# An attention and two-MoE kernel on one core: first transposes copied ahead of later angles, and w_out and g used unsplit in the first token block

## The chip, the cores and the metric

The kernel runs on one core of a Trainium2 chip. The metric is device time in microseconds of one execution, smaller is better. A run before the change took 1125.24 us (median of 3 runs, 1124.36 to 1126.98). The engines that matter here are PE (TensorE, matmuls and transposes), DVE (VectorE), ACT (ScalarE), POOL (GpSimd) and SP, which issues most of the DMAs.

## The reference

Inputs are float32. Three stages follow one another; the output of one, seen as 3072 tokens by 384 features, is the input of the next.

```
# 1. attention with complex decay, per batch (4) and head (8), 768 steps, head_dim 48
S = a_norm[t] * S + outer(k[t], v[t])      # a_norm complex, magnitude capped at 0.999
y[t] = q[t] @ real(S)
# 2. first MoE layer, d_ff = 2048
h = x @ w_in
g = h * tanh(log1p(exp(min(h, 20))))       # mish
x2 = g @ w_out
# 3. second MoE layer, d_ff = 1536
out = ((x2 @ w_a) * (x2 @ w_b)) @ w_out2
```

## The kernel before, in words

**Tiling.** Tokens are worked in 6 blocks of 512 (128 time steps of each of the 4 batches). Attention is done in 24 chunks of 128 steps, numbered so that chunks 0 to 3 make block 0, chunks 4 to 7 block 1, and so on. The angles and decays of a chunk are summed by matmuls against a triangle (`csum`, `tsum`), turned into sines and exponentials on ACT, multiplied into q and k on DVE (`rotate`), transposed on PE (`transpose_one`, copied out of PSUM by ACT), multiplied to scores, masked on DVE (L384) and multiplied with v.

**The lead.** `lead_in` (L754) does chunks 0 to 3 before any other work. The order of its instructions is a list written out by hand (L793 to L805); `in_order` then pins that order on DVE, ACT, PE and POOL. In it `(tr, c)` is the transposes of chunk c with their copies, `(trig, c)` two sines on ACT, `(reduced, c)` three DVE instructions that bring the summed angle into a turn, `(rotate, c)` two DVE multiplies, `(decode, None)` and `(split, None)` the first piece of w_in, `(decode_2, None)` and `(split_2, None)` the first piece of w_out.

**Weights.** Weights come as 768 KB pieces of two 32-bit words per number. `decode` (L152) makes float32 of them by three DVE instructions. `split` (L160) makes two float32r tiles: ACT copies the float32 tile into the high part, POOL subtracts it from the whole to get the low part. w_in and w_out have 8 pieces each, numbered j; each serves two of the 16 feature tiles f. They are loaded while block 0 runs, in turn (in 0, out 0, in 1, ...).

**First MoE.** For each block and each f, `moe1_h` makes `hps` = w_in by x with 9 matmuls (3 slices of 384 features, times 3 terms: high by high, high by low, low by high). `mish_factor` (L532) is one DVE instruction and four on ACT. `mish_product` (L542) multiplies by h on DVE, giving m; then `gh`, the high part of m, is made by ACT in the first and last block and by DVE in the others, and `gl`, the low part, by DVE in the first and last block and by POOL in the others. `moe1_x2` (L556) adds w_out by g into three PSUM tiles, again with 3 terms of 3 matmuls each, two units of f later. The accumulated tiles of a block are copied out as `x2o` after f = 15.

**What sets the order.** Outside the lead, instructions are recorded in the order of the loop over units (b, f) at L835, the attention chunks 4 to 23 in slots spread over it (`run_to`), and a scheduler of the framework then chooses, engine by engine, the order in the queues. Each engine's queue is in order.

**Second MoE.** `moe2_ab`, `moe2_mul`, `moe2_out`, with the same three terms. Its weights are loaded by `prep` from the last units of block 4 on. The first `EARLY` = 2 sets of them have tiles of their own, the rest reuse the tiles of the first MoE's weights (`shared`, L169), which lie in two pools of 16.

Of the kernel before, what the change touches and what calls it, by code (L numbers as in the profile page):

```python
# [21 lines left out]
def kernel(  # L22
# [14 lines left out]
    nc = tc.nc  # L37
# [77 lines left out]
    allp = ctx.enter_context(ExitStack())  # L115
    xp = allp.enter_context(tc.tile_pool(name="xp", bufs=2))
    ps_a = allp.enter_context(tc.tile_pool(name="ps_a", bufs=3, space=PSUM))
    wps = [allp.enter_context(tc.tile_pool(name="wp0", bufs=NF))]
    right = allp.enter_context(ExitStack())
    w1 = allp.enter_context(ExitStack())  # L120
    ps_h = w1.enter_context(tc.tile_pool(name="ps_h", bufs=2, space=PSUM))
# [14 lines left out]

    weights = {}

    def load_weights(nm, j, src, pool, place):


        a, b = src.shape[1:]
        if src.dtype == F32:
            raw = pool.tile([P, a, b], F32, tag="wraw", name="wraw", bufs=2)
            nc.sync.dma_start(out=raw, in_=src)
        else:
            b //= 2
            raw = pool.tile([P, a, b, 2], U32, tag="wraw", name="wraw", bufs=2)
            nc.sync.dma_start(out=raw.rearrange("p a b t -> p a (b t)"), in_=src)
        f = [raw]  # L150

        def decode():  # L152
            if src.dtype != F32:
                f[0] = pool.tile([P, a, b], F32, tag="wf32", name="wf32")
                fu, low, high = f[0].bitcast(U32), raw[..., 0], raw[..., 1]
                nc.vector.tensor_scalar(fu, high, 3, 0x3FFFFFFF, ALU.logical_shift_left, ALU.bitwise_and)
                nc.vector.scalar_tensor_tensor(fu, high, 0xC0000000, fu, ALU.bitwise_and, ALU.bitwise_or)
                nc.vector.scalar_tensor_tensor(fu, low, 29, fu, ALU.logical_shift_right, ALU.bitwise_or)

        def split():  # L160
            hi, lo = weights[nm, j] = [place(f"w{nm}{i}{j}", [P, a, b]) for i in "hl"]
            act(out=hi, in_=f[0], func=AF.Copy)
            nc.gpsimd.tensor_tensor(lo, f[0], hi.bitcast(F32), ALU.subtract)  # L163

        return [decode, split]

    taken = [0]

    def shared(name, shape):  # L169

        pool = wps[taken[0] // NF % 2]
# [367 lines left out]
        act(out=m, in_=m, func=AF.Exp, scale=-1.0)  # L539
        return m  # L540

    def mish_product(p, m, on_act):  # L542

        nc.vector.scalar_tensor_tensor(m, m, 2.5, p, ALU.subtract, ALU.mult)  # L544
        gh = mp.tile([P, TN], F32R, tag="gh", name="gh")
        gl = mp.tile([P, TN], F32R, tag="gl", name="gl")
        if on_act:
            act(out=gh, in_=m, func=AF.Copy)
        else:
            nc.vector.tensor_copy(gh, m)  # L550
        (nc.vector if on_act else nc.gpsimd).tensor_tensor(gl, m, gh.bitcast(F32), ALU.subtract)  # L551
        return gh, gl

    x2ps = {}

    def moe1_x2(blk, f, gh, gl):  # L556
        for m in range(KM):
            if f == 0:
                x2ps[m] = ps_x.tile([P, TN], F32, tag=f"x{m}", name=f"x2ps{m}")
            ms = slice(m * P, (m + 1) * P)  # L560
            hi, lo = w_row("out", f)
            for i, (w, g) in enumerate([(hi, gh), (hi, gl), (lo, gh)]):
                nc.tensor.matmul(  # L563
                    x2ps[m], lhsT=w[:, ms], rhs=g,
                    start=(f == 0 and i == 0), stop=(f == NF - 1 and i == 2),
                )
        if f == NF - 1:
            for m in range(KM):
                t = mp.tile([P, TN], F32, tag="m", name="x2o")
                if m == 1:  # L570
                    nc.vector.tensor_scalar(t, x2ps[m], -0.4, None, ALU.mult)
                else:
                    act(out=t, in_=x2ps[m], func=AF.Copy, scale=-0.4)
                nc.sync.dma_start(out=x2_d[blk][m * P:(m + 1) * P, :], in_=t)
# [4 lines left out]
    def load_w2(early):  # L579


        for j in range(NF2 // 2):
            def place(name, shape, j=j):
                return early[0].tile(shape, F32R, name=name) if j < EARLY else shared(name, shape)

            for nm, src in (("a", wcols(w2_a, j)), ("b", wcols(w2_b, j)), ("o", wrow(w2_out, j))):
                yield lambda nm=nm, j=j, src=src, place=place: load_weights(nm, j, src, wst, place)
# [166 lines left out]
    def lead_in():  # L754
# [38 lines left out]
        for fn, c in (  # L793
            (decay_1, 0), (decay_2, 0), (decay_1, 1), (decay_3, 0), (decay_2, 1), (decay_1, 2), (tan_ell, 0),
            (decay_3, 1), (sum_ell, 0), (decay_2, 2), (sizes, 0), (tan_ell, 1), (decay_1, 3), (decay_3, 2),
            (sum_ell, 1), (decay_2, 3), (sizes, 1), (tan_ell, 2), (decay_3, 3), (sum_ell, 2), (sizes, 2), (tan_ell, 3), (sum_ell, 3),
            (scale_qk, 0), (sizes, 3), (scale_qk, 1), (decode, None), (split, None),
            (angle, 0), (angle, 1), (angle, 2), (angle, 3), (turned, 0), (turned, 1), (turned, 2), (turned, 3),
            (scale_qk, 2), (reduced, 0), (trig, 0), (reduced, 1), (trig, 1), (rotate, 0), (reduced, 2), (trig, 2),
            (tr, 0), (rotate, 1), (scale_qk, 3), (sc, 0), (tr, 1), (reduced, 3), (trig, 3), (values, 0), (rotate, 2),  # L800
            (store_y, 0), (sc, 1), (tr, 2), (read_x, 0), (split_x, 0), (rotate, 3), (values, 1), (decode_2, None),
            (store_y, 1), (sc, 2), (tr, 3), (lambda: run_to(0), None), (read_x, 1), (split_x, 1), (values, 2),
            (split_2, None), (store_y, 2), (lambda: run_to(1), None), (sc, 3), (read_x, 2), (split_x, 2),
            (lambda: run_to(2), None), (values, 3), (store_y, 3), (read_x, 3), (split_x, 3),
        ):  # L805
            fn() if c is None else fn(c)
# [28 lines left out]
    for ui in range(len(units) + lag):  # L835
        if ui == 3:
            behind(after_lead, last)
        if ui < len(units):
            blk, f = units[ui]
            if f == 0:  # L840
                base = slot[0]
                want = ends[blk + 1] if blk + 1 < NB else n_slots
                if blk == NB - 1:
                    make_room()
            p = moe1_h(blk, f, ps_a if blk == NB - 1 and f % 2 else ps_h)
            do_w()
            run_to(base + (want - base) * (2 * f + 1) // (2 * NF))
            m = mish_factor(p)
            if blk == NB - 1 and f % 5 != 4 or blk == NB - 2 and f >= NF - 2:
                next(prep, None)  # L850
        if ui == 1:
# [224 lines left out]
```

## Time and profile before

| what | value |
|---|---|
| median of 3 runs | 1125.24 us |
| the profiled execution, time | 1126.85 us |
| the profiled execution, span | 1125.1 us |
| PE busy | 1063.6 us (95%) |
| PE weight loads busy | 897.1 us (80%) |
| DVE busy | 663.9 us (59%) |
| ACT busy | 617.7 us (55%) |
| POOL busy | 228.8 us (20%) |
| first matmul of block 0 (`hps`) | 63.26 us |
| first copy of block 0's result (`x2o`) | about 209 us |

The time of a run includes some microseconds around the span. Busy PE counts overlapping, modelled ends of matmuls, so a busy PE may still have room; the busy time of the weight loads is the better sign of how dense the matmuls are. The stretches used below are the lead (0 to 63.26 us), block 0 of the first MoE with the weights' arrival and the chunks 4 to 8 (63.26 to 209.20 us), block 1 (209.20 to 301.50 us) and a stretch of the same kind after it.

### The profile page before, as it was taken

How to read it: one execution, taken by the hardware profiler on the slowest of the kernel's cores; microseconds unless marked ns; L12 is line 12 of the kernel's file. 1: busy time of each engine (PE TensorE's matmuls, PEld its weight loads, DVE VectorE, ACT ScalarE, POOL GpSimd, SP SyncE). 2: the span in 40 equal slices, each digit the busy share in tenths (PEclk: the TensorE clock that was granted, in tenths of full speed). 3: DMA queues.
4: the chain of work that ended last, by engine and by line, in shares of the span. 5: the costliest groups of instructions: out<-in, count | busy, mean ns of one | idle time of the engine just before them, and what ended most of it. 6: DMA issues, size and time to landing. Idle time of an engine off the chain costs nothing.

```text
span 1125.1 us, 15347 instructions
## 1 busy us (share of the span) xinstructions
PE 1063.6 (95%) x5788; PEld 897.1 (80%) x5788; DVE 663.9 (59%) x1014; ACT 617.7 (55%) x978; POOL 228.8 (20%) x220
## 2 busy tenths in 40 slices
PE   3897988999999999999998999999999999999997
PEld 1775667888788878878876778878888888888886
DVE  5789988777677767677658998742232321412222
ACT  6578877877787887879766862221121121211211
POOL 2022324343334334334232212100000000000000
PEclk9898989999999999999999999999999999999999
DMA  9335755733343453324325556410010100100000
GB/s 207 73 106 129 177 127 129 161 64 64 65 97 74 82 119 68 65 64 99 71 71 165 164 181 202 130 57 1 1 57 1 29 29 1 43 1 1 29 1 30
DMA packets 203545, 90.87 MB, mean 81 GB/s; under 512 B 144781, under 2 KB 187850, under 8 KB 203466
## 3 DMA queue, kind: packets, MB, share of 16 engines
q1 hardware_dynamic: 203450, 89.82, 32.6%
q8 instruction: 47, 0.77, 0.3%
q14 instruction: 32, 0.26, 0.1%
q10 hardware_dynamic: 16, 0.01, 0.0%
HBM read 72.44 MB, written 17.36 MB: 80 GB/s over the span
## 4 chain that ended last, share of the span: by engine, by line
PE 43%; ACT 12%; DVE 10%; issue 9%; DMA 4%; POOL 3%; SPq 0%; ACTq 0%; POOLq 0%; DVEq 0%
PE ops L641 11%; PE psa L616 11%; PE psb L616 11%; ACT m L60 7%; PE hps L529 4%; PE x2ps L563 3%; DVE m L535 2%; DVE kh L349 1%; ACT s L60 1%; ACT L55 1%; DMA look<-in_a_im_dram 1%; POOL wbl L163 1%; ACT a L60 1%; DVE m L544 1%; PE py L404 1%
## 5 line engine op out<-in xcount | busy, mean ns | idle before, releaser
L627 DVE TENSOR_TENSOR a_sb<-a_sb,psb 128x512 f32<-128x512 f32 x72 | 49.4, 686 | 221.7 <-PE psb L616 220.1
L60 ACT ACTIVATE m<-m 128x512 f32<-128x512 f32 x192 | 120.2, 628 | 67.8 <-DVE m L535 65.3
L60 ACT ACTIVATE ph<-a_sb 128x512 fp32r<-128x512 f32 x72 | 45.5, 632 | 178.4 <-DVE a_sb L627 178.4
L529 PE MATMUL hps<-xh,winh 128*128 128x512 f32 x288 | 119.5, 416 | 8.7 <-DVE m L544 6.9
L60 ACT ACTIVATE a_sb<-psa 128x512 f32<-128x512 f32 x72 | 42.9, 596 | 151.6 <-PE psa L616 149.4
L563 PE MATMUL x2ps<-gl,wouth 128*128 128x512 f32 x288 | 114.9, 399 | 4.8 <-DVE gl L551 3.4
L529 PE MATMUL hps<-xl,winh 128*128 128x512 f32 x288 | 116.4, 404 | 0.5 <-DMA xl<-yt_dl 0.5
L563 PE MATMUL x2ps<-gh,wouth 128*128 128x512 f32 x288 | 114.8, 406 | 1.4 <-ACT x2o L60 0.8
L529 PE MATMUL hps<-xh,winl 128*128 128x512 f32 x288 | 114.9, 399 | 0.0
L551 POOL TENSOR_TENSOR gl<-m,gh 128x512 fp32r<-128x512 f32 x64 | 83.4, 1303 | 154.6 <-DVE gh L550 147.1
L563 PE MATMUL x2ps<-gh,woutl 128*128 128x512 f32 x288 | 113.2, 393 | 0.0
L641 PE MATMUL ops<-woh,ph 128*128 128x384 f32 x288 | 97.2, 337 | 0.0
L641 PE MATMUL ops<-woh,pl 128*128 128x384 f32 x288 | 97.2, 337 | 0.0
L641 PE MATMUL ops<-wol,ph 128*128 128x384 f32 x288 | 96.8, 336 | 0.0
L544 DVE SCALAR_TENSOR_TENSOR m<-m,hps 128x512 f32<-128x512 f32 x96 | 65.4, 682 | 40.5 <-ACT m L60 40.5
L616 PE MATMUL psa<-xh,wah 128*128 128x512 f32 x216 | 84.7, 392 | 2.2 <-DVE a_sb L627 2.2
L616 PE MATMUL psa<-xh,wal 128*128 128x512 f32 x216 | 85.1, 394 | 0.0
L616 PE MATMUL psa<-xl,wah 128*128 128x512 f32 x216 | 85.0, 394 | 0.0
L616 PE MATMUL psb<-xh,wbh 128*128 128x512 f32 x216 | 84.5, 391 | 0.0
L616 PE MATMUL psb<-xh,wbl 128*128 128x512 f32 x216 | 84.4, 391 | 0.0
L616 PE MATMUL psb<-xl,wbh 128*128 128x512 f32 x216 | 84.4, 391 | 0.0
L535 DVE TENSOR_SCALAR m<-hps 128x512 f32<-128x512 f32 x96 | 65.5, 682 | 17.8 <-PE hps L529 16.3
(137 smaller groups left out, 2322.1 us busy)
## 6 DMA issues: line engine op xcount, KB each, us to landing
wraw<-in_moe_w_out_dram SPq DMA_DIRECT2D x14, 768.0 KB
wraw<-in_moe_w_in_dram SPq DMA_DIRECT2D x8, 768.0 KB
a<-in_a_re_dram SPq DMA_DIRECT2D x24, 192.0 KB
a<-in_a_im_dram SPq DMA_DIRECT2D x24, 192.0 KB
q<-in_q_dram SPq DMA_DIRECT2D x24, 192.0 KB
k<-in_k_dram SPq DMA_DIRECT2D x24, 192.0 KB
v<-in_v_dram SPq DMA_DIRECT2D x24, 192.0 KB
wraw<-in_moe_w_a_dram SPq DMA_DIRECT2D x6, 768.0 KB
```

What stands on the lines that cost most here:

```text
L55: load = nc.scalar.preload_act_table_set(name)
L60: x = nc.scalar.activation(**kw)
L163: nc.gpsimd.tensor_tensor(lo, f[0], hi.bitcast(F32), ALU.subtract)
L349: eng.tensor_tensor(tile1(c, nm + "h", [P, H, 2, D]), x, w, ALU.mult)
L529: nc.tensor.matmul(p, lhsT=w[:, kk, :], rhs=x[:, kk, :], start=(i == 0), stop=(i == len(ops) - 1))
L535: nc.vector.tensor_scalar(m, p, 20.0, None, ALU.min)
L544: nc.vector.scalar_tensor_tensor(m, m, 2.5, p, ALU.subtract, ALU.mult)
L551: (nc.vector if on_act else nc.gpsimd).tensor_tensor(gl, m, gh.bitcast(F32), ALU.subtract)
L563: nc.tensor.matmul(x2ps[m], lhsT=w[:, ms], rhs=g, start=(f == 0 and i == 0), stop=(f == NF - 1 and i == 2),)
L616: nc.tensor.matmul(p, lhsT=w[:, kk, :], rhs=x[:, kk, :], start=(i == 0), stop=(i == len(ops) - 1))
L627: nc.vector.tensor_tensor(a_sb, a_sb, pb, ALU.mult)
L641: nc.tensor.matmul(ops_t[t], lhsT=x[:, tsl], rhs=w, start=(f == 0 and i == 0), stop=(f == NF2 - 1 and i == 2),)
```

## The change

Three things change.

First, the hand-written order of the lead. `(tr, 0)` stands before `(reduced, 2)` and `(trig, 2)`, so ACT copies chunk 0's transposes before it takes chunk 2's sines. `(decode_2, None)` stands after `(rotate, 2)` and no longer after `(rotate, 3)`, and `(rotate, 3)` stands before the read of chunk 0's result.

Second, block 0 uses g and w_out whole. `mish_product` writes one float32 tile for block 0, without gh and gl, and `moe1_x2` makes one float32 matmul per 128 output features in place of three float32r ones. w_out is decoded into tiles that stay (`whole`), and is split only in block 1, one piece at every even f.

Third, the tiles follow. The first pool holds 8 tiles for split weights and 9 for whole ones; a w_out low part and the second set of w2 weights take places of the latter. `EARLY` is 1.

```diff
-    wps = [allp.enter_context(tc.tile_pool(name="wp0", bufs=NF))]
+    wps = [allp.enter_context(tc.tile_pool(name="wp0", bufs=NF // 2))]
...
         def decode():
+            if late:
+                f[0] = wps[0].tile([P, a, b], F32, tag="f", name=f"w{nm}{j}", bufs=NF // 2 + 1)
+                whole[nm, j] = f[0], split
...
         def split():
-            hi, lo = weights[nm, j] = [place(f"w{nm}{i}{j}", [P, a, b]) for i in "hl"]
+            hi = place(f"w{nm}h{j}", [P, a, b])
+            if late:
+                lo = wps[0].tile([P, a, b], F32R, tag="f", name=f"w{nm}l{j}", bufs=NF // 2 + 1)
+            else:
+                lo = place(f"w{nm}l{j}", [P, a, b])
+            weights[nm, j] = [hi, lo]
             act(out=hi, in_=f[0], func=AF.Copy)
             nc.gpsimd.tensor_tensor(lo, f[0], hi.bitcast(F32), ALU.subtract)

-        return [decode, split]
+        return [decode, lambda: None] if late else [decode, split]
...
-    def mish_product(p, m, on_act):
+    def mish_product(p, m, blk):
+        if not blk:
+            g = mp.tile([P, TN], F32R, tag="gh", name="gh").bitcast(F32)
+            nc.vector.scalar_tensor_tensor(g, m, 2.5, p, ALU.subtract, ALU.mult)
+            return [g]
+        on_act = blk == NB - 1
...
-            hi, lo = w_row("out", f)
-            for i, (w, g) in enumerate([(hi, gh), (hi, gl), (lo, gh)]):
+            if len(g) == 1:
+                terms = [(whole["out", f // 2][0][:, f % 2, :], g[0])]
+            else:
+                (hi, lo), (gh, gl) = w_row("out", f), g
+                terms = [(hi, gh), (hi, gl), (lo, gh)]
...
-            (scale_qk, 2), (reduced, 0), (trig, 0), (reduced, 1), (trig, 1), (rotate, 0), (reduced, 2), (trig, 2),
-            (tr, 0), (rotate, 1), (scale_qk, 3), (sc, 0), (tr, 1), (reduced, 3), (trig, 3), (values, 0), (rotate, 2),
-            (store_y, 0), (sc, 1), (tr, 2), (read_x, 0), (split_x, 0), (rotate, 3), (values, 1), (decode_2, None),
-            (store_y, 1), (sc, 2), (tr, 3), (lambda: run_to(0), None), (read_x, 1), (split_x, 1), (values, 2),
+            (scale_qk, 2), (reduced, 0), (trig, 0), (reduced, 1), (trig, 1), (rotate, 0), (tr, 0), (reduced, 2),
+            (trig, 2), (rotate, 1), (scale_qk, 3), (sc, 0), (tr, 1), (reduced, 3), (trig, 3), (values, 0), (rotate, 2),
+            (decode_2, None), (store_y, 0), (sc, 1), (rotate, 3), (tr, 2), (read_x, 0), (split_x, 0), (values, 1), (store_y, 1),
+            (sc, 2), (tr, 3), (lambda: run_to(0), None), (read_x, 1), (split_x, 1), (values, 2),
...
-    EARLY = 2
+    EARLY = 1
...
+            if blk == 1 and f % 2 == 0:
+                whole["out", f // 2][1]()
...
-            ready[ui] = mish_product(p, m, blk in (0, NB - 1))
+            ready[ui] = mish_product(p, m, blk)
```

In ACT's queue in the lead, `turn_d` is the handing over of a chunk's angle, `size<-a` a chunk's two sines, `qT` and `kT` the copies of its transposes. Before, from the sines of chunk 1 on:

```order
L60 ACTIVATE size<-a 128x384
L60 ACTIVATE size<-a,bias_hpi 128x384
L317 DMA turn_d_93<-a 1x384
L60 ACTIVATE size<-a 128x384
L60 ACTIVATE size<-a,bias_hpi 128x384
L60 ACTIVATE qT_128<-pqT 96x512
L60 ACTIVATE qT_129<-pqT 96x512
L60 ACTIVATE kT<-pkT 96x512 x2
```

And now, from the same place:

```order
L60 ACTIVATE size<-a 128x384
L60 ACTIVATE size<-a,bias_hpi 128x384
L60 ACTIVATE qT_128<-pqT 96x512
L60 ACTIVATE qT_129<-pqT 96x512
L60 ACTIVATE kT<-pkT 96x512 x2
L332 DMA turn_d_93<-a 1x384
L60 ACTIVATE size<-a 128x384
L60 ACTIVATE size<-a,bias_hpi 128x384
```

The four copies moved ahead of the handing over and the sines of chunk 2.

On PE in block 0, `x2ps` are the three accumulators of the first MoE's result. Before, the first unit's matmuls were these nine:

```order
L563 MATMUL x2ps_768<-gh,wouth_531 128x512
L563 MATMUL x2ps_772<-gh,wouth_531 128x512
L563 MATMUL x2ps_768<-gl,wouth_531 128x512
L563 MATMUL x2ps_768<-gh,woutl_532 128x512
L563 MATMUL x2ps_772<-gl,wouth_531 128x512
L563 MATMUL x2ps_772<-gh,woutl_532 128x512
L563 MATMUL x2ps_776<-gh,wouth_531 128x512
L563 MATMUL x2ps_776<-gl,wouth_531 128x512
L563 MATMUL x2ps_776<-gh,woutl_532 128x512
```

Now there are three, of float32, between the last matmul of one `hps` and the first of the next:

```order
L544 MATMUL hps<-xh,winl_612 128x512
L587 MATMUL x2ps_754<-gh,wout_407 128x512
L587 MATMUL x2ps_756<-gh,wout_407 128x512
L587 MATMUL x2ps_758<-gh,wout_407 128x512
L544 MATMUL hps<-xh,winh_611 128x512
```

Nine matmuls per unit became three; the `hps` ones around them are as before.

On POOL, where w_in's and w_out's low parts (`winl`, `woutl`) are subtracted, they took turns before, in the first half of block 0:

```order
L163 TENSOR_TENSOR winl_276<-wf_271,winh_275 128x768
L163 TENSOR_TENSOR woutl_532<-wf_468,wouth_531 128x768
L218 MEMSET v 128x16
L163 TENSOR_TENSOR winl_616<-wf_599,winh_615 128x768
L163 TENSOR_TENSOR woutl_653<-wf_619,wouth_652 128x768
L163 TENSOR_TENSOR winl_749<-wf_656,winh_748 128x768
L163 TENSOR_TENSOR woutl_804<-wf_752,wouth_803 128x768
```

Now the w_out ones follow the last w_in one, near the end of block 0; `sh<-size` is the high part of chunk 8's decay, `W` a chunk's state:

```order
L178 TENSOR_TENSOR winl_1409<-wf_1340,winh_1408 128x768
L178 TENSOR_TENSOR woutl_1711<-wout_407,wouth_1710 128x768
L178 TENSOR_TENSOR woutl_1835<-wout_615,wouth_1834 128x768
L178 TENSOR_TENSOR woutl_1974<-wout_738,wouth_1973 128x768
L178 TENSOR_TENSOR woutl_2101<-wout_837,wouth_2100 128x768
L178 TENSOR_TENSOR woutl_2235<-wout_982,wouth_2234 128x768
L286 TENSOR_SCALAR sh<-size 128x384
L178 TENSOR_TENSOR woutl_2362<-wout_1132,wouth_2361 128x768
```

The splits are recorded in block 1, but stand in the queues of ACT and POOL before block 0 ends: the eight `wouth` copies on ACT come after the eleventh to fourteenth unit of block 0.

## Rows read from the trace of the kernel before

**Rows 1.** Stretches: bounds, length, each engine's busy us, granted clock, DMA, GB/s.

```profile
0.00:63.26 63.26, 38.79 (x234) 31.28 (x235) 38.28 (x71) 38.53 (x65) 9.37 (x25) 0.95 0.74 135
63.26:209.20 145.94, 128.06 (x753) 101.68 (x753) 128.39 (x190) 116.31 (x182) 42.89 (x32) 0.93 0.57 137
209.20:301.50 92.30, 90.60 (x572) 75.85 (x573) 65.58 (x105) 74.85 (x120) 37.97 (x39) 1.00 0.41 87
301.50:400.00 98.50, 97.55 (x622) 81.99 (x621) 70.93 (x113) 79.64 (x126) 37.45 (x40) 1.00 0.38 81
```

**Rows 2.** Waits in block 0: engine, line, releaser, total us, times, longest.

```profile
PE hps L529 <- DVE m L544: 6.9, 5, 4.5
DVE m L535 <- PE hps L529: 7.5, 4, 3.7
DVE wf L156 <- POOL winl L163: 2.9, 2, 1.7
```

**Rows 3.** PE and DVE in the lead, in order of time: start, us, what.

```profile
32.12 1.04 PE L362 MATMUL pkT<-ident,kh 128*96 128x128 f32 x8
35.92 3.71 PE L380 MATMUL psc<-qT,kT 96*128 96x128 f32 x16 [2.76 <-ACT kT L60]
...
45.77 0.73 DVE L384 COPY_PREDICATED am<-csum,psc 128x512 f32<-128x512 int32 x1 [2.14 <-PE psc L380]
...
51.76 0.55 DVE L156 TENSOR_SCALAR wf<-wraw 128x768 uint32<-128x768 uint32 x1
...
54.22 1.35 DVE L384 COPY_PREDICATED am<-csum,psc 128x512 f32<-128x512 int32 x2
```

**Rows 4.** ACT in the lead, in order of time.

```profile
33.30 0.52 ACT L60 ACTIVATE size<-a 128x384 f32<-128x384 f32 x1 [2.16 <-DVE a L309]
...
34.24 1.05 ACT L60 ACTIVATE qT<-pqT 96x512 f32<-96x512 f32 x2
35.19 1.07 ACT L60 ACTIVATE kT<-pkT 96x512 f32<-96x512 f32 x2
```

**Rows 5.** A stretch of the lead, columns as in rows 1.

```profile
36.00:42.80 6.80, 6.80 (x32) 6.63 (x33) 3.81 (x8) 2.02 (x4) 0.00 (x0) 0.50 0.80 146
```

**Rows 6.** Groups in block 0: line, operation, count, busy us, mean ns, idle before.

```profile
L551 DVE TENSOR_TENSOR gl<-m,gh 128x512 fp32r<-128x512 f32 x16 | 12.5, 781 | 0.0
L251 DVE SCALAR_TENSOR_TENSOR size<-r,s 128x384 f32<-128x384 f32 x6 | 6.8, 1133 | 0.1
L60 ACT ACTIVATE gh<-m 128x512 fp32r<-128x512 f32 x16 | 10.0, 626 | 3.5 <-DVE m L544 3.4
L60 ACT ACTIVATE wouth<-wf 128x768 fp32r<-128x768 f32 x7 | 5.9, 836 | 1.6 <-DVE wf L158 1.6
L163 POOL TENSOR_TENSOR woutl<-wf,wouth 128x768 fp32r<-128x768 f32 x7 | 13.5, 1923 | 39.6 <-ACT wouth L60 28.9 <-DMA wraw<-in_moe_w_out_dram 10.7
```

**Rows 7.** PE in block 0, in order of time.

```profile
69.93 0.81 PE L284 MATMUL pt<-a,tsum 128*128 128x384 f32 x2
70.58 4.20 PE L439 MATMUL pu<-v,kh 128*96 128x48 f32 x48
...
82.38 0.39 PE L563 MATMUL x2ps<-gl,wouth 128*128 128x512 f32 x1
82.61 0.39 PE L563 MATMUL x2ps<-gh,woutl 128*128 128x512 f32 x1
...
90.96 1.65 PE L284 MATMUL pl<-size,csum 128*128 128x384 f32 x2 [1.30 <-DVE size L251]
91.83 1.20 PE L529 MATMUL hps<-xl,winh 128*128 128x512 f32 x1
```

**Rows 8.** A DVE instruction beside a POOL one, and a DVE group in the lead.

```profile
120.31 2.18 DVE L262 SCALAR_TENSOR_TENSOR a<-size,a 1x384 f32<-1x384 f32 x1
119.61 2.47 POOL L163 TENSOR_TENSOR woutl<-wf,wouth 128x768 fp32r<-128x768 f32 x1 [5.38 <-ACT wouth L60]
L251 DVE SCALAR_TENSOR_TENSOR size<-r,s 128x384 f32<-128x384 f32 x5 | 2.8, 558 | 0.2
```

More of the change, by code (lines that the diff above doesn't have):

```diff
@@ L137, with load_weights @@
     weights = {}
-    def load_weights(nm, j, src, pool, place):
+    whole = {}
+    def load_weights(nm, j, src, pool, place, late=False):
         a, b = src.shape[1:]
@@ L152, in decode @@
         def decode():
+            if late:
+                f[0] = wps[0].tile([P, a, b], F32, tag="f", name=f"w{nm}{j}", bufs=NF // 2 + 1)
+                whole[nm, j] = f[0], split
+                if src.dtype == F32:
+                    nc.vector.tensor_copy(f[0], raw)
+                    return
             if src.dtype != F32:
-                f[0] = pool.tile([P, a, b], F32, tag="wf32", name="wf32")
+                if not late:
+                    f[0] = pool.tile([P, a, b], F32, tag="wf32", name="wf32")
                 fu, low, high = f[0].bitcast(U32), raw[..., 0], raw[..., 1]
@@ L160, in split @@
         def split():
-            hi, lo = weights[nm, j] = [place(f"w{nm}{i}{j}", [P, a, b]) for i in "hl"]
+            hi = place(f"w{nm}h{j}", [P, a, b])
[4 more added lines that the diff above has]
+            weights[nm, j] = [hi, lo]
             act(out=hi, in_=f[0], func=AF.Copy)
             nc.gpsimd.tensor_tensor(lo, f[0], hi.bitcast(F32), ALU.subtract)
-        return [decode, split]
+        return [decode, lambda: None] if late else [decode, split]
     taken = [0]
     def shared(name, shape):
-        pool = wps[taken[0] // NF % 2]
+        pool = wps[taken[0] % (3 * NF // 2) >= NF // 2]
         taken[0] += 1
@@ L554, with moe1_x2 @@
     x2ps = {}
-    def moe1_x2(blk, f, gh, gl):
+    def moe1_x2(blk, f, *g):
         for m in range(KM):
@@ L560, in moe1_x2 @@
             ms = slice(m * P, (m + 1) * P)
-            hi, lo = w_row("out", f)
-            for i, (w, g) in enumerate([(hi, gh), (hi, gl), (lo, gh)]):
+            if len(g) == 1:
[3 more added lines that the diff above has]
+                terms = [(hi, gh), (hi, gl), (lo, gh)]
+            for i, (w, x) in enumerate(terms):
                 nc.tensor.matmul(
-                    x2ps[m], lhsT=w[:, ms], rhs=g,
-                    start=(f == 0 and i == 0), stop=(f == NF - 1 and i == 2),
+                    x2ps[m], lhsT=w[:, ms], rhs=x,
+                    start=(f == 0 and i == 0), stop=(f == NF - 1 and i == len(terms) - 1),
                 )
@@ L583, in place @@
             def place(name, shape, j=j):
+                if j == EARLY:
+                    return wps[0].tile(shape, F32R, tag="f", name=name, bufs=NF // 2 + 1)
                 return early[0].tile(shape, F32R, name=name) if j < EARLY else shared(name, shape)
@@ L726, in pipeline @@
             yield
-    steps1 = [lambda nm=nm, j=j, src=src: load_weights(nm, j, src, wst, shared) for nm, j, src in wq]
+    steps1 = [lambda nm=nm, j=j, src=src: load_weights(nm, j, src, wst, shared, nm == "out") for nm, j, src in wq]
     weights1 = None
```

## The prediction

> **What bounds the kernel now.** I read the busy times by stretch first, then the groups and waits inside the stretch that stands out, then the order of time in the lead. In the stretch after block 1, PE is busy 97.55 of 98.50 us while DVE has 70.93 and ACT 79.64 [rows 1]: PE sets the pace there, and nothing that only frees DVE or ACT can help. Block 0 is different. It takes 145.94 us, against 92.30 for block 1, with the same 288 matmuls of the first MoE; DVE is busy 128.39 us of it (88%), ACT 116.31, and PE and DVE wait for each other in turn, 6.9 and 7.5 us [rows 1, 2]. PE's 128.06 there is swollen by overlapping ends and by slow clock. A better size comes from the weight loads: 81.99 us of loads go with 97.55 us of dense PE [rows 1], so 101.68 us of loads stand for 101.68 x 97.55 / 81.99 = 121 us. The granted clock was 0.93, so if it has two levels, 1.2 and 2.4 GHz, about 14% or 20 us were at the lower one, and 10 us of the 121 are lost to that. PE's work in block 0 at full clock is thus about 111 us: it has some 35 us to give, DVE only 17.5, ACT 30. Before block 0 lie 63.26 us of lead, in which no engine is busy for more than 39 [rows 1]: there a chain of waits sets the end.
>
> **The lead.** Chunk 0's kT transposes end at 32.12 + 1.04 = 33.16, but ACT first takes chunk 2's sines, which wait 2.16 us for DVE and start at 33.30; the copies run from 34.24 to 36.26, and the scores start at 35.92, after 2.76 us of waiting [rows 3, 4]. With the copies ahead, three of the four can be made while PE still transposes, the last some 0.6 us after 33.16, so the scores start at about 33.8: 2.1 us earlier. The sines come later by about 1 us (rotate 2, which needs them, has that time, since DVE first masks the scores and reduces chunk 3's angle). From 36.00 to 42.80 PE ran at a granted clock of 0.50, the lower level, with no gap at all [rows 5], after the 2.76 us wait. If the wait shrinks the clock may stay up and the 6.8 us of work take 3.4; how much of that would reach the end is open, since DVE is then late, so I count 0 and keep 3.4 as the upper end.
>
> The decode of w_out's first piece took from 51.76 to 54.22, 2.46 us, between chunk 3's rotation and chunk 2's mask [rows 3]; PE needs that mask for the values. Its new place is the 2.14 us in which DVE waited ahead of the mask at 45.77 [rows 3]. It overfills the hole by 0.3 us, so the net is 2.1. Together 4.2 us; I take 4, with 0 (something else, such as a copy or the chunk 3 chain, ends just as late) and 8 (4.2 + 3.4) as ends. The decode in its old place also held the raw buffer, so w_out's second piece is fetched earlier too; nothing waited for it in the lead, so I count nothing.
>
> **Block 0, what goes.** On DVE 16 gl subtractions, 12.5 us; on ACT 16 gh copies, 10.0 us [rows 6]. One decode of w_a, which the scheduler had placed inside block 0, now falls later: 2.5 us less for DVE by the same 2.46. The eight wouth copies and woutl subtractions do not leave block 0, though they are recorded in block 1: the queues hold them before its end, at 0.84 us each on ACT and 1.92 each on POOL [rows 6]. One of the eight was in the lead before, so ACT gains one copy in block 0. DVE goes from 128.4 to about 113.5, ACT from 116.3 to about 107.
>
> **Block 0, what comes.** PE makes 48 float32 matmuls 128x512 in place of 144 float32r ones. A float32r one follows the last after 82.61 - 82.38 = 0.23 us, so three are 0.69. No float32 matmul of that width is in the trace. The nearest is the angle sum, 128x384, in two records: at full clock the next instruction starts 70.58 - 69.93 = 0.65 us after it, which scaled by 512/384 is 0.87 us; at a lower clock, 91.83 - 90.96 = 0.87 us, scaled 1.16 [rows 7]. The lowest price would be two records at the float32r pace, 0.46. I take 0.87, the row that PE's clock in a fuller block 0 resembles: 48 x (0.87 - 0.69) = +9 us; the ends are 48 x (0.46 - 0.69) = -11 and 48 x (1.16 - 0.69) = +23.
>
> In the Trainium skill, the page "Perfetto Trace Analysis", section "Engine Utilization", a note halves the array's output rate for FP32_LOW_HIGH; read for a whole float32 matmul, 128x512 elements at half of the 307.2 G elements/s of its table would be an estimated 0.43 us, and PE would lose 12 us of work instead of gaining 9. The 0.65 us of the 128x384 one speaks for a quarter of the rate, and I go by that.
>
> **The sum.** After the change the loads in block 0 are PE 111 + 9 = 120 us, DVE 113.5, ACT 107. Before, the fullest engine had 128.4 of 145.9 us, 88%; where PE alone sets the pace it fills 99% [rows 1]. With three engines this close to each other I take 90% for PE: 120 / 0.90 = 133 to 134 us, 12 less. Blocks 1 to 5 do the same work with PE as the bound: nothing; the new tiles hold the same low parts, each place freed a block before it is written again. In the second MoE's weights three steps are made a few units later than before, each still units ahead of its first use: nothing, plus or minus 2 us. The sum is -4 - 12 = -16 us on the profiled execution's 1126.85 us (span 1125.1 and about 1.7 around it), which is 1.6 us above the median. Against the median, 1125.24 - 16 = 1109 us.
>
> **The rivals.**
>
> *PE takes over in block 0.* Its waits are not only for DVE's throughput but for chains (product, copy, mask, transposes), and each float32 group is 2.6 us that nothing can pass in PE's queue. Then the 9 us of added matmuls lie on the path, and the freed 12.5 us of DVE give only that much back, plus some 3 us from the shorter chain behind the product: block 0 loses 3 us, the lead 4, and it takes 1118. For it: PE goes to 120 at full clock, 131 with today's clock losses. Against it: PE has 35 us to give.
>
> *More than the sum.* PE in block 0 fills up to 98% and stays at the upper clock, so block 0 takes about 122 us, 24 less; with the lead -28, or 1097; half of it, 1102, is more likely. For it: gl and gh are also links of the chain to PE. Against it: the startup of block 0, where weights still arrive, stays.
>
> *No change.* The lead's chain ends as late as before (0), and PE takes over with the 1.16 us price: +23 - 12.5 - 10 in the best overlap, about 0: 1125.
>
> *Slower, by the burst on POOL and ACT.* Eight woutl of 1.84 to 1.92 us now stand almost in a row near the end of block 0, 15 us of POOL, and chunk 8's `sh` stands behind five of them, 9.4 us. DVE's low part of the same sum waits for `sh`, and everything behind it on DVE, masks and products included, waits too. What is more, a DVE instruction beside such a subtraction took 2.18 us (it ended with the POOL one at 122.1 to 122.5), and a group with two inputs in SBUF has a mean of 1133 ns in block 0 where it had 558 in the lead [rows 6, 8]: by the 2.18 less some 0.56, up to 1.6 us for each woutl, 13 us for eight. If the wait for `sh` (9.4 us) and half of the blocking (6.5) come out on PE's path, together with 9 us of float32 matmuls no longer hidden, that is 25 us against the 16 gained and some 4 that a block 0 without the burst could still give: +5, 1130. It decides from the point where POOL runs more than about 16 us behind what DVE asks for. Against it: before, the same subtractions blocked DVE one at a time, seven of them in block 0, so most of the 13 us is paid already; and the gl instructions that were also hit are gone.
>
> The page "SBUF — State Buffer" of the Trainium skill, section "Who interferes with whom", says that a DVE instruction with two SBUF inputs and a GpSimd one share a port pair that one of them holds for its whole duration while the other stands still. The 2.18 us row agrees; by it the burst costs no more in all than the same eight one by one, as long as DVE has other instructions to make.
>
> **How the numbers follow.** A measurement here tells apart about 0.2%, 2.2 us. I give the sum (1104 to 1115) 0.58, PE taking over 0.17, more than the sum 0.12, no change 0.06, slower 0.07. So faster 0.87, same 0.06, slower 0.07. The range 1100 to 1120 holds the sum, PE taking over and half of the more favourable case, 0.81; 1120 is also the sum with the lead and half of block 0's gain gone, and 1100 is the sum with the full clock gain of the lead and a block 0 that gives 5 us more.
>
> **What would show it.** The scores of chunk 0 start near 33.8 and not 35.92, with a granted clock above 0.5 right after; the decode of w_out ends ahead of chunk 1's mask; the first `hps` starts near 59. The float32 matmuls of block 0 follow one another after 0.87 us in two records each. The first `x2o` comes near 193, some 16 us earlier, DVE's busy time between is near 113, and the later stretches keep their lengths. The prediction is wrong if `hps` in block 0 waits longer than before, if the float32 matmuls take over 1 us, if DVE stands still behind the `sh` of chunk 8, or if PE waits in the first units of the second MoE for weights.

## The result and the profile after

The changed kernel takes **1109.43 us** (median of 4 runs, 1108.54 to 1112.84) against 1125.24: a ratio of 0.9857, 95% interval 0.9835 to 0.9879. The forecast was 1109, so the total is right. Its parts are not all right, and the rest of this text is about them. The profiled execution took 1108.67 us with a span of 1107.0, 18.1 less than the span before; single profiles are compared below, so the parts add up to 18.1 and not to 15.8.

The stretches of the changed kernel, columns as in [rows 1]: the lead up to the first `hps`, block 0 up to the first `x2o`, block 1 up to the next block's `x2o`, and the window of [rows 5].

```profile
0.00:58.44 58.44, 36.55 (x234) 28.26 (x235) 37.98 (x71) 37.76 (x64) 7.41 (x24) 1.00 0.77 146
58.44:196.52 138.08, 127.80 (x700) 90.58 (x699) 119.36 (x173) 107.40 (x165) 43.61 (x33) 0.96 0.57 145
196.52:296.91 100.39, 99.22 (x624) 82.35 (x623) 71.33 (x114) 80.94 (x128) 38.32 (x40) 1.00 0.37 80
...
36.00:42.80 6.80, 5.80 (x51) 5.30 (x49) 6.66 (x11) 3.81 (x8) 0.00 (x0) 1.00 0.94 150
```

The lead lost 4.8 us, block 0 7.9 (145.97 to 138.08). The later `x2o` stand 10 to 11 us earlier than before for blocks 1 to 4, so blocks 1 to 3 gave 2.5 us back; from there to the end another 8 come in. Part of this lies in the mark. Before, ACT was busy and copied the first `x2o` after PE had made block 0's last matmul; now it copies while four of them (0.43 us each) are still to come. On PE, the first instruction behind those matmuls is this one, before and now:

```profile
209.09 0.44 PE L404 MATMUL py<-qT,W 128*64 128x128 f32 x4
198.13 0.44 PE L419 MATMUL py<-qT,W 128*64 128x128 f32 x4
```

So for PE block 0 lost 6.1 us (145.8 to 139.7), and blocks 1 to 3 gave back 0.8. The runs below that are made from the changed kernel have the mark where it has it.

The clock column tells as much as the lengths. While PE has work, a stretch of length L with a mean granted clock c has lost about L x (1 - c) against the upper of the two levels (2.4 and 1.2 GHz): before, 3.2 us in the lead and 10.2 in block 0; now none in the lead and 5.5 in block 0. With 1.7 us at 602 to 612 us (clock 0.83 before, 1.00 now), that is an estimated 9.6 of the 18.1 us.

**The lead.** PE, then ACT, then DVE of the changed kernel, in order of time, against [rows 3, 4]:

```profile
32.28 1.04 PE L377 MATMUL pkT<-ident,kh 128*96 128x128 f32 x8
33.82 2.02 PE L395 MATMUL psc<-qT,kT 96*128 96x128 f32 x16 [0.49 <-ACT kT L60]
```

```profile
33.08 0.59 ACT L60 ACTIVATE kT<-pkT 96x512 f32<-96x512 f32 x1
33.42 0.20 ACTq L332 DMA_DIRECT2D turn_d<-a  x1
33.55 0.60 ACT L60 ACTIVATE kT<-pkT 96x512 f32<-96x512 f32 x1
34.03 0.53 ACT L60 ACTIVATE size<-a 128x384 f32<-128x384 f32 x1
```

```profile
42.13 0.96 DVE L168 SCALAR_TENSOR_TENSOR wout<-wraw,wout 128x768 uint32<-128x768 uint32 x1
43.01 1.34 DVE L399 COPY_PREDICATED am<-csum,psc 128x512 f32<-128x512 int32 x2
```

The scores start at 33.82 as forecast, after 0.49 us of waiting in place of 2.76, and take 2.02 us in place of 3.71: the clock stays up. The decode ends where the mask can start.

**Block 0.** Float32 matmuls on PE:

```profile
127.86 2.74 PE L587 MATMUL x2ps<-gh,wout 128*128 128x512 f32 x6
130.43 0.81 PE L299 MATMUL pl<-size,csum 128*128 128x384 f32 x2
```

Three matmuls are six records, and what follows starts 2.57 us later: 0.86 us each, against the 0.87 that was scaled up from [rows 7]. DVE's busy time is 119.4, not 113.5. Two groups of w_out's decode show most of the difference; w_in's decode in the same block has means of 0.55 (L166) and 0.95 (L167):

```profile
L167 DVE SCALAR_TENSOR_TENSOR wout<-wraw,wout 128x768 uint32<-128x768 uint32 x7 | 9.7, 1380 | 0.1
L166 DVE TENSOR_SCALAR wout<-wraw 128x768 uint32<-128x768 uint32 x7 | 7.1, 1014 | 0.0
```

They stand beside POOL's subtractions. Another 2.5 us are the decode of w_a's first piece, which the forecast had put behind block 0: it starts at 153.40, inside it. Six of the eight `woutl` make a burst in the second half of block 0 (POOL, in order of time, then DVE):

```profile
142.97 6.83 POOL L178 TENSOR_TENSOR woutl<-wout,wouth 128x768 fp32r<-128x768 f32 x3 [0.34 <-ACT wouth L60]
150.25 1.95 POOL L178 TENSOR_TENSOR woutl<-wout,wouth 128x768 fp32r<-128x768 f32 x1 [0.45 <-POOL woutl L178]
153.57 0.75 POOL L286 TENSOR_SCALAR sh<-size 128x384 fp32r<-128x384 f32 x1 [1.37 <-DVE size L266]
154.29 1.81 POOL L178 TENSOR_TENSOR woutl<-wout,wouth 128x768 fp32r<-128x768 f32 x1
```

```profile
143.44 2.20 DVE L166 TENSOR_SCALAR wout<-wraw 128x768 uint32<-128x768 uint32 x1
145.67 2.44 DVE L167 SCALAR_TENSOR_TENSOR wout<-wraw,wout 128x768 uint32<-128x768 uint32 x1
...
150.41 2.60 DVE L168 SCALAR_TENSOR_TENSOR wout<-wraw,wout 128x768 uint32<-128x768 uint32 x1
...
153.40 0.55 DVE L166 TENSOR_SCALAR wf<-wraw 128x768 uint32<-128x768 uint32 x1
154.35 2.17 DVE L288 TENSOR_TENSOR sl<-size,sh 128x384 fp32r<-128x384 f32 x1 [0.41 <-POOL sh L286]
```

Each of the DVE instructions of 2.17 us and more takes 1.5 to 1.7 us more than its kind does elsewhere (0.55 or 0.95), and the two that can be followed end about their own length after a subtraction does: at 153.01 after one that ends at 152.20, at 156.52 after one at 156.10. DVE stood still beside POOL. PE of the same stretch, and the window behind it:

```profile
154.58 0.74 PE L299 MATMUL pl<-sh,csum_r 128*128 128x384 f32 x1
156.57 0.44 PE L299 MATMUL pl<-sl,csum_r 128*128 128x384 f32 x1 [1.26 <-DVE sl L288]
158.50 0.80 PE L544 MATMUL hps<-xh,winh 128*128 128x512 f32 x1 [1.49 <-DVE gh L561]
159.09 0.63 PE L544 MATMUL hps<-xl,winh 128*128 128x512 f32 x1
159.52 0.63 PE L544 MATMUL hps<-xh,winl 128*128 128x512 f32 x1
```

```profile
158.50:164.90 6.40, 6.40 (x20) 5.33 (x21) 5.41 (x8) 3.73 (x8) 2.02 (x2) 0.53 0.68 193
```

PE waits 1.26 us for the late `sl`, 1.49 for the product that stood behind it (`gh` is block 0's whole g), and then runs 6.4 us at a granted clock of 0.53, nearly all at the lower level: matmuls start 0.43 us apart, not 0.23. That is 2.8 us of waits and 3 us of clock.

### The profile page after: what moved, and what is told of

Its sections match the earlier page's. It is cut to its first block, busy times and chain, and to the rows that moved or that the text cites. A ratio compares the mean times of both kernels' runs of the same rounds, so it can differ in the third digit from the quotient of the medians.

```text
span 1107.0 us, 15213 instructions
## 1 busy us (share of the span) xinstructions
PE 1060.1 (96%) x5740; PEld 882.8 (80%) x5740; DVE 658.1 (59%) x998; ACT 607.7 (55%) x962; POOL 226.7 (20%) x220
## 4 chain that ended last, share of the span: by engine, by line
PE 73%; DVE 12%; ACT 8%; issue 4%; DMA 2%; POOL 0%; SPq 0%; ACTq 0%; DVEq 0%; POOLq 0%
PE ops L667 14%; PE psa L642 13%; PE psb L642 13%; PE hps L544 12%; PE x2ps L587 11%; ACT m L60 4%; PE psc L395 3%; PE py L419 2%; PE pu L454 2%; DVE m L550 2%; PE pqT L377 1%; PE pkT L377 1%; DVE m L564 1%; ACT s L60 1%; ACT L55 1%
## 5 line engine op out<-in xcount | busy, mean ns | idle before, releaser
L587 PE MATMUL x2ps<-gl,wouth 128*128 128x512 f32 x240 | 94.8, 395 | 2.2 <-DVE gl L571 1.1
L587 PE MATMUL x2ps<-gh,wouth 128*128 128x512 f32 x240 | 93.9, 404 | 2.3 <-ACT gh L60 1.9
L587 PE MATMUL x2ps<-gh,woutl 128*128 128x512 f32 x240 | 93.8, 391 | 0.0
L564 DVE SCALAR_TENSOR_TENSOR m<-m,hps 128x512 f32<-128x512 f32 x80 | 54.5, 683 | 37.1 <-ACT m L60 37.0
L655 DVE TENSOR_TENSOR pl<-a_sb,ph 128x512 fp32r<-128x512 f32 x72 | 52.3, 726 | 38.9 <-ACT ph L60 38.9
```

Of the source, the lines that this page charges most:

```text
L587: nc.tensor.matmul(x2ps[m], lhsT=w[:, ms], rhs=x, start=(f == 0 and i == 0), stop=(f == NF - 1 and i == len(terms) - 1),)
L655: nc.vector.tensor_tensor(lo, a_sb, hi.bitcast(F32), ALU.subtract)
```

## The experiments

Each batch has its own runs of the kernel before (medians 1126.12, 1127.34 and 1126.95 us); ratios are to those. "Distance" is first `hps` to first `x2o`, block 0. Lengths of stretches come from one profiled execution of each kernel.

**The lead alone**: the new order in the kernel before.

```diff
-            (scale_qk, 2), (reduced, 0), (trig, 0), (reduced, 1), (trig, 1), (rotate, 0), (reduced, 2), (trig, 2),
+            (scale_qk, 2), (reduced, 0), (trig, 0), (reduced, 1), (trig, 1), (rotate, 0), (tr, 0), (reduced, 2),
...
-            (store_y, 0), (sc, 1), (tr, 2), (read_x, 0), (split_x, 0), (rotate, 3), (values, 1), (decode_2, None),
+            (decode_2, None), (store_y, 0), (sc, 1), (rotate, 3), (tr, 2), (read_x, 0), (split_x, 0), (values, 1), (store_y, 1),
```

> The kernel before with the new order of the lead alone. Theory (the lead is a chain of waits; what is gained there stays, since PE is the bound from block 1 on): first hps at 58.4 us as in the changed kernel, 4.8 us earlier, and 1120.5 us, ratio 0.996. Rival 1 (block 0 is bound by DVE and by weights that arrive, and swallows the lead's gain): first hps just as early, but the first x2o at most 1 us earlier, 1125 us. Rival 2 (the gain in the lead needs the w_out tiles that stay, because the decode would wait for a buffer): hps not before 61 us.

1122.24 us, ratio 0.9969 (0.995 to 0.9987). First `hps` at 59.63 (58.4 was expected), first `x2o` 2.9 us and the later ones 2.9 to 3.9 us earlier. The lead's gain is real and stays, at 3 to 4 us.

**EARLY alone**: `EARLY = 1` in the kernel before.

```diff
-    EARLY = 2
+    EARLY = 1
```

> The kernel before with EARLY = 1 alone: only the second set of w2 weights takes shared tiles instead of its own. Theory (the 5 to 7 us that the changed kernel gains behind block 4 come from the later weight steps, which this edit makes as well): the first x2o at 209 us as before, the stretch from the last block on shorter by 5 to 7 us, 1119 us, ratio 0.995. Rival 1 (that gain comes with the whole tiles of w_out, or with where the earlier part happens to end): no change, 1125 us. Rival 2 (the tiles come free too late and PE waits for weights in the first units of the second MoE): slower by 2 us or more.

1119.01 us, ratio 0.9934 (0.9909 to 0.996): the part counted at 0 gives some 7 us (4.5 to 10 by the interval). From block 4's `x2o` to unit 18 of the second MoE it takes 175.6 us; before 181.6, changed kernel 175.0. So the late gain is this edit's. Two pieces of it can be seen (columns as in [rows 1]; first the kernel before, then this one):

```profile
602.00:612.00 10.00, 10.00 (x38) 8.08 (x38) 8.23 (x12) 5.57 (x10) 0.00 (x0) 0.83 0.48 154
742.00:752.00 10.00, 8.09 (x39) 6.65 (x37) 6.00 (x13) 1.12 (x2) 0.00 (x0) 1.00 0.17 47
```

```profile
602.00:612.00 10.00, 9.11 (x38) 6.77 (x39) 10.00 (x14) 5.10 (x9) 1.84 (x1) 1.00 0.59 191
742.00:752.00 10.00, 10.00 (x49) 8.66 (x48) 3.48 (x6) 3.33 (x6) 0.00 (x0) 1.00 0.34 112
```

A stretch at lower clock is gone (1.7 us), and PE no longer stands still near 744 us (1.9 us), where before it waited for DVE, which itself had waited 8.9 us for `grow<-good_d`, a DMA. That wait of DVE is still there in this run, 8.6 us up to 732.6; it no longer reaches PE, and why is not shown. The other 2 to 3 us were not found.

**The old lead in the changed kernel.**

```diff
-            (scale_qk, 2), (reduced, 0), (trig, 0), (reduced, 1), (trig, 1), (rotate, 0), (tr, 0), (reduced, 2),
+            (scale_qk, 2), (reduced, 0), (trig, 0), (reduced, 1), (trig, 1), (rotate, 0), (reduced, 2), (trig, 2),
...
-            (decode_2, None), (store_y, 0), (sc, 1), (rotate, 3), (tr, 2), (read_x, 0), (split_x, 0), (values, 1), (store_y, 1),
+            (store_y, 0), (sc, 1), (tr, 2), (read_x, 0), (split_x, 0), (rotate, 3), (values, 1), (decode_2, None),
```

> The changed kernel with the old order of the lead. Theory (lead, block 0 and the later part add up): first hps at 63.3 us, the distance from it to the first x2o about 138 us as in the changed kernel, 1109.4 + 4.8 = 1114.2 us, ratio to before 0.990. Rival (block 0's gain needs the early start of w_out's second piece that the new lead gives): distance 142 us or more, 1118 us.

1114.13 us, ratio 0.990 (0.9871 to 0.993); first `hps` at 61.8 and not 63.3, distance 138.5, so the rival fell. The lead and the rest add up within the noise. Block 0's edit was not run alone. By difference it gives some 5 of the 16 us: the changed kernel takes 1.43% off, the lead alone 0.31, `EARLY` alone 0.66, which leaves 0.46%, give or take some 4 us.

**Half of the float32 work on PE.**

```diff
+                n = TN // 2 if len(g) == 1 and 0 < f < NF - 1 else TN
                 nc.tensor.matmul(
-                    x2ps[m], lhsT=w[:, ms], rhs=x,
+                    x2ps[m][:, :n], lhsT=w[:, ms], rhs=x[:, :n],
```

> The changed kernel, but in block 0 the float32 matmuls of f = 1 to 14 take 256 of the 512 tokens only (the other half of block 0's result is left out for these f): 42 matmuls of 0.87 us become 0.44, PE has 18 us less to do in block 0, no other engine less. Theory (in block 0 DVE with its locks and waits sets the pace and PE's 9 added us are hidden): the distance from the first hps to the first x2o stays at 138 us within 3, 1108 to 1109. Rival (PE is the bound of block 0 after the change): the distance falls by 9 us or more, 1100 or less.

1101.13 us, ratio 0.9775 (0.9741 to 0.981); distance 129.1, 9 less. That is 42 matmuls by half of 0.86, 18 us of PE work, of which half comes out. My theory that PE has room for it fell, and the rival's "PE is the bound" holds for half of the work taken away.

**The splits held back.** Each `wouth` copy is put behind the last exponential of its unit in block 1, in ACT's queue; the subtraction follows it.

```diff
+            x = act(out=hi, in_=f[0], func=AF.Copy)
+            if late:
+                tc.add_manual_dep(x.ins, held[0].ins.name, no_sync, reason="split in block 1")
...
+        held[0] = act(out=m, in_=m, func=AF.Exp, scale=-1.0)
```

> The changed kernel, but each copy of a w_out high part stands in ACT's queue behind the last exponential of the unit of block 1 in which it is recorded, so the eight splits are spread over block 1 and none is in block 0. Theory (the burst of eight subtractions on POOL and eight copies on ACT costs little, since DVE pays for a lock once in either place): block 0 shorter by 0 to 3 us, block 1 longer by as much, the time within 2 us of the changed kernel, 1108 to 1111. Rival 1 (the burst blocks DVE and holds back chunk 8's sums): block 0 shorter by 5 us or more and the time 4 us less. Rival 2 (PE in block 1 then waits for the low parts): block 1 longer by 4 us or more, slower.

1103.66 us (1103.17 to 1106.04), ratio 0.9787 (0.9759 to 0.9814). Blocks 0 and 1 here, and PE at the place of the stall:

```profile
58.70:191.19 132.49, 125.56 (x699) 89.06 (x699) 113.64 (x173) 102.87 (x159) 29.79 (x26) 0.97 0.59 151
191.19:291.44 100.25, 98.81 (x624) 82.22 (x623) 76.25 (x114) 85.78 (x134) 57.55 (x48) 1.00 0.37 80
```

```profile
155.36 0.74 PE L303 MATMUL pl<-sh,csum_r 128*128 128x384 f32 x1
155.94 0.34 PE L303 MATMUL pl<-sl,csum_r 128*128 128x384 f32 x1
156.12 0.39 PE L548 MATMUL hps<-xh,winh 128*128 128x512 f32 x1
156.35 0.40 PE L548 MATMUL hps<-xl,winh 128*128 128x512 f32 x1
```

Both waits and the slow clock behind them are gone, and so are the long DVE instructions: at this place `sl` takes 0.55 us, the decode's three 0.54, 0.96 and 0.95. Block 0 is 5.6 us shorter, DVE is busy 113.6 us, and block 1, where POOL now works 57.6 us in place of 38.3, is no longer. Rival 1 holds. At its place the burst cost more than these 5.6 us, because this run lost more to the clock ahead of it (3.4 us at 69.5 to 77 us, mean 0.54) than the changed kernel did (1.7 at 82 to 86, 0.58). From the first DVE instruction of the eleventh unit (`m<-hps`) to that of the fourteenth the changed kernel takes 28.3 us, this one 21.0 and the next run 23.1 (columns as in [rows 1], in this order):

```profile
135.70:164.00 28.30, 23.97 (x125) 16.52 (x125) 25.80 (x32) 21.32 (x33) 17.80 (x11) 0.89 0.48 136
137.40:158.40 21.00, 20.06 (x119) 14.12 (x118) 18.58 (x32) 16.52 (x25) 6.98 (x5) 1.00 0.67 173
135.30:158.40 23.10, 21.58 (x119) 15.27 (x118) 18.31 (x31) 21.00 (x32) 5.67 (x5) 0.93 0.64 167
```

So the burst cost 7.3 us at its place, 5.6 in the block.

**Only POOL's subtractions held back**, the copies left in the burst.

```diff
-            nc.gpsimd.tensor_tensor(lo, f[0], hi.bitcast(F32), ALU.subtract)
+            x = nc.gpsimd.tensor_tensor(lo, f[0], hi.bitcast(F32), ALU.subtract)
+            if late:
+                tc.add_manual_dep(x.ins, held[0].ins.name, behind_act, reason="low part in block 1")
```

> The changed kernel, with each of the eight w_out subtractions on POOL tied behind the last exponential of its unit in block 1, while the eight ACT copies of the high parts stay where they were, in the burst near units 10 to 12 of block 0. Holding both back had shortened the stretch from the first hps to the first x2o from 138.1 to 132.5 us and given 1103.7. Theory (the burst costs by POOL: DVE instructions stand still beside the subtractions, and chunk 8's sh stands behind them): most of it comes back without moving a copy, the stretch is 133 to 134 us and the time 1103 to 1106. Rival (the burst costs by the 6.5 us of copies in ACT's queue, in front of the exponentials that lead to the product): nothing comes back, the stretch is 137.5 to 139 us and the time 1108 to 1111. Half of each would be 135 to 136 us and about 1107.

1109.24 us, ratio 0.9839 (0.9821 to 0.9856): the time says rival, the place says theory. Blocks 0 and 1, and then POOL and PE in block 1:

```profile
58.28:191.22 132.94, 126.06 (x700) 89.78 (x699) 112.77 (x173) 107.24 (x165) 29.24 (x25) 0.97 0.60 151
191.22:295.71 104.49, 99.38 (x624) 82.50 (x623) 73.20 (x114) 80.92 (x128) 51.82 (x49) 1.00 0.36 77
```

```profile
227.42 1.82 POOL L181 TENSOR_TENSOR woutl<-wout,wouth 128x768 fp32r<-128x768 f32 x1 [4.46 <-ACT m L60]
229.33 0.51 POOL L291 TENSOR_SCALAR sh<-a 128x384 fp32r<-128x384 f32 x1
```

```profile
229.89 0.44 PE L304 MATMUL pt<-sh,csum_r 128*128 128x384 f32 x1 [1.23 <-POOL sh L291]
```

Block 0 is 5.1 us shorter with every copy in place, and at the burst's place 5.2 of the 7.3 us are back. So most of the burst's cost is POOL's. Some 1.6 of the other 2.1 are lower clock (0.93 in the row above); that the copies on ACT cost nothing is not shown. Block 1 gives 4.1 away again: a subtraction at the head of POOL's queue waits 4.46 us for its exponential, `sh` stands behind it, and PE waits for `sh` (3.7 us in three places).

**Both parts held, and w_in's low parts on DVE.** First the second edit alone, then both.

```diff
-            nc.gpsimd.tensor_tensor(lo, f[0], hi.bitcast(F32), ALU.subtract)
+            (nc.vector if nm == "in" and j else nc.gpsimd).tensor_tensor(lo, f[0], hi.bitcast(F32), ALU.subtract)
```

> The changed kernel, but DVE instead of POOL makes the low parts of w_in's pieces 1 to 7, so POOL subtracts nothing beside the decodes. Theory (the lock between DVE and POOL took 8 us of DVE's gain): the decodes of w_out fall back to 0.55, 0.95 and 0.95 us each, 8 us in all, other two-input instructions lose some 3 us of blocking, and the seven subtractions add 7 x 0.95 = 6.7 us: DVE's busy time in block 0 goes from 120.6 to about 116, block 0 is 2 to 5 us shorter, the time 1105 to 1107. Rival (DVE's queue does not set the pace): within 1 us of the changed kernel.

1107.52 us (1106.46 to 1117.38), ratio 0.9847 (0.9807 to 0.9887), distance 137.0, 1.1 less. The theory asked for 2 to 5, and the interval holds the changed kernel's ratio, so no gain is shown. The burst is still there, from the eleventh unit to the fourteenth and on PE:

```profile
133.20:162.80 29.60, 23.35 (x129) 15.22 (x127) 28.19 (x34) 21.78 (x34) 14.99 (x10) 1.00 0.54 141
```

```profile
155.38 0.44 PE L299 MATMUL pl<-sl,csum_r 128*128 128x384 f32 x1 [1.36 <-DVE sl L288]
157.31 0.50 PE L544 MATMUL hps<-xh,winh 128*128 128x512 f32 x1 [1.49 <-DVE gh L561]
```

PE has the same two waits as in the changed kernel, but the granted clock stays at 1.00, and the stretch is still 29.6 us, against 21.2 (132.3 to 153.5) in the next run, which has no burst. So a burst costs as much without the lower clock, by more waits of PE, which speaks against counting the 3 us of clock above as a cost of their own.

> The changed kernel with both parts of the w_out split held back into block 1 (that alone gave 1103.7, a stretch from first hps to first x2o of 132.5 us, and 28.6 us of POOL in block 0), and DVE makes the low parts 1 to 7 of w_in in place of POOL. Theory (with the burst gone PE's own work and chains set block 0, so whom a low part is made by hardly matters): 1102 to 1105, the stretch within 1.5 us of 132.5. Rival A (what is left is DVE standing still beside POOL's seven w_in subtractions, 1.84 us each, 13 us in all, of which DVE would pay some 0.95 each itself): the stretch loses 4 to 6 us, 1098 to 1100. Rival B (DVE's queue is the tight one, each added instruction of about 0.95 us lies on the path): the stretch is 6 us longer, 1109 to 1110.

**1101.47 us** (1099.83 to 1103.78), ratio 0.9776 (0.9757 to 0.9795), the fastest of the kernels that compute everything, 8 us below the changed kernel; its interval overlaps that of the splits held alone. Block 0:

```profile
58.26:186.26 128.00, 123.68 (x700) 88.43 (x699) 112.04 (x180) 103.28 (x159) 15.28 (x19) 0.99 0.63 156
```

Rival A holds for the place, though its time, 1098 to 1100, was not reached: 4.5 us less than with the splits alone, some 2 of them by the clock (0.99 against 0.97). DVE makes seven instructions more (0.945 us each) and is busy 1.6 us less. What it no longer pays is standing still beside POOL: w_out's decodes (L168, L169) have means of 0.55 and 0.95 us, where they had 0.78 and 1.17 with the splits alone.

**DVE's decodes.** Two runs on what the blocked decodes cost: w_out's decode made to wait for POOL's w_in subtraction, as it had to before; and one of three decode instructions left out for pieces 1 to 7.

```diff
+                if late and j:
+                    tc.add_manual_dep(x.ins, winl[0].ins.name, behind_pool, reason="decode after the low part")
```

> The changed kernel, but the decode of each w_out piece in block 0 waits until POOL has made the low part of the w_in piece before it. Theory (block 0 gained 8 us and not 12 because the decodes, freed of their old wait for the one float32 buffer, now run beside POOL's subtractions and are blocked: their three instructions have means of 1014, 1380 and 1183 ns where the w_in ones have 552, 947 and 949): the three means fall to 0.56, 0.95 and 0.95 us, DVE's busy time in block 0 from 120.6 to about 113, and the time falls by 1 to 4 us, to 1106 to 1108. Rival 1 (blocked or waiting is the same for DVE, whose queue is in order): the means fall, but idle time takes their place and the time stays within 1 us. Rival 2 (PE is the bound in block 0): means fall, DVE has more idle time, same time.

1109.58 us, ratio 0.9853 (0.9827 to 0.9878), distance 138.7: unchanged, as rival 1 has it, and the theory's 1106 to 1108 was missed. DVE is busy 113.3 us, but waits as long for `winl`:

```profile
DVE wout L168 <- POOL winl L182: 7.0, 4, 1.8
```

The granted clock of its block 0 is 0.99, though, so the same length holds some 4 us less loss by the clock, and its block 1 takes 104.0 us in place of 100.4 in this profile: PE waits 0.74 and 1.20 us for the next tokens' DMAs, and the granted clock of 280 to 296 us is 0.79. The run can't say that waiting is free.

```diff
-                nc.vector.scalar_tensor_tensor(fu, high, 0xC0000000, fu, ALU.bitwise_and, ALU.bitwise_or)
+                if not late or not j:
+                    nc.vector.scalar_tensor_tensor(fu, high, 0xC0000000, fu, ALU.bitwise_and, ALU.bitwise_or)
```

> The changed kernel, but the decode of w_out's pieces 1 to 7 leaves out one of its three DVE instructions (the one that sets the sign): DVE has 7 x 0.95 to 1.38, 7 to 10 us, less to do in block 0, PE nothing less. Theory (DVE sets the pace there): the distance from the first hps to the first x2o falls by 5 to 9 us, time 1101 to 1105. Rival (PE sets it, or chains of waits that a shorter DVE queue doesn't shorten): 2 us or less, 1108.

1109.83 us, ratio 0.9838 (0.9803 to 0.9872). Distance 135.0, 3.1 less, between theory and rival; block 2 then takes 104.4 us where the changed kernel takes 99.4. PE there, and the window from that point:

```profile
381.58 0.50 PE L545 MATMUL hps<-xh,winh 128*128 128x512 f32 x1 [0.53 <-DMA xh<-yt_dh]
...
384.14 0.80 PE L545 MATMUL hps<-xl,winh 128*128 128x512 f32 x1 [1.43 <-DMA xl<-yt_dl]
```

```profile
384.20:390.30 6.10, 6.10 (x18) 4.85 (x19) 1.03 (x3) 1.65 (x4) 3.19 (x3) 0.50 0.08 3
```

At the end of a block PE waits for the next tokens' DMAs; here it was followed by 6 us at the lower level, 3 us lost, where the changed kernel's clock is 1.00 at every block's end. So in this profile (1111.16 us) the gain was not hidden but lost again later. That the four runs' median lost it in the same way is not shown.

## Why the prediction was right, point by point

- **Lead, -4: right** (-4.8 in the trace, 3 to 4 alone). The scores' start, the copies' times and the decode's place came as worked out. The clock gain that was counted 0 came in the rows (3.2 us), but little of it reached the end: the sum without it was 4.2.
- **Float32 matmul, 0.87 us: right** (0.86). By the half-rate note of the Trainium skill, "Perfetto Trace Analysis", section "Engine Utilization", read for a whole float32 matmul, it would have been an estimated 0.43; the trace does not agree.
- **Block 0, -12: wrong by a third** (-7.9, and -6.1 by PE's mark). The step that failed is the fill of 90% over 120 us of PE work, with DVE at 113.5 beside it: it took the eight splits as costless, since each had been paid before. The burst cost 5.6 us of the block, by `sl`, the product behind it and PE's waits for both. With the splits held back the distance is 132.5, and 120 / 132.5 is 90.6%. The 90% itself was a choice: with w_in's low parts on DVE as well it is 120 / 128.0, 93.7%.
- **Two readings behind it were wrong.** The 92.30 us set against block 0 hold 268 matmuls of the first MoE and not 288; a whole block 1, from first `x2o` to first `x2o`, took 99.0 us (209.23 to 308.20). Block 0 still stands out. And w_a's decode, 2.5 us of DVE, did not leave block 0 (it starts at 153.40). A slip without weight: halfway from 1109 to 1097 is 1103, not 1102.
- **The rival "slower, by the burst"** had place and mechanism right (`sh`, `sl`, blocked DVE instructions) and its price at least twice too high: 15.9 us for the burst in the working (9.4 + 6.5; the 25 also hold 9 of float32 matmuls), 7.3 measured at the place. What the forecast inferred, that a burst costs no more in all than the same eight one by one, is refuted by the held splits: spread over block 1 they cost nothing that shows. The rule itself, in the Trainium skill's "SBUF — State Buffer", section "Who interferes with whom", that one engine holds the shared port pair for a whole instruction, agrees with the four long DVE rows above (2.17 to 2.60 us).
- **The rival "PE takes over"** is half true: of 18 us of float32 matmuls taken away, 9 came out.
- **Blocks 1 to 5, 0: about right** (2.5 us given back in blocks 1 to 3, of which 1.7 lie in the mark and 0.8 are not explained; block 5 is part of the late gain).
- **Second MoE's weights, 0 plus or minus 2: wrong** by some 6 us. I asked whether each set is ready ahead of its first use, and it is; I did not ask what the old order made late, namely PE's slow stretch near 602 us and its stall near 744. How `EARLY` removes them is not shown.

So the total was right because 4 us too much in block 0 and 2.5 given back behind it met 8 us too little at the end, some 6 of them by `EARLY`. The range was sized for the first, and held the second by luck.

## What to carry to other kernels

Work that is recorded later may still stand where its inputs are ready: if it is moved off a turn-taking resource, ask where it will bunch, and pin it if the bunch meets an engine that shares something with it. After a wait on PE look at what the clock does, which here cost as much again in some runs and nothing in another, and compare stretches by length and granted clock together. A gain in one stretch can be lost again at the next place where PE waits, so judge an edit by its place and by the total, both.

## What was not expected of the hardware

- Two waits of PE close together were followed by a stretch at the lower clock level that cost as much as they did or more: 1.26 + 1.49 us and then 6.4 us at 0.53; at 381 to 384 us, 0.53 + 1.43 and then 6.1 us at 0.50. It does not always follow: after 1.36 + 1.49 us, in the run with only w_in's low parts on DVE, the clock stayed at 1.00. In all, by L x (1 - c), the lower level cost 15 us of the span before (3.2 + 10.2 + 1.7) and 5.5 now.
- Not only DVE instructions with two inputs in SBUF are held up, as the forecast counted: L166, with one, took 2.20 us beside a subtraction on POOL and 0.55 elsewhere.
- A subtraction of 128x768 took 1.84 us on POOL and 0.945 on DVE.
